# One-bank PSUM tiles, P·V in runs of three, and new costs in the planner of an LSH-attention and feed-forward kernel

## The chip, the cores and the metric

The kernel runs on one core of a Trainium2 chip. The metric is the device time of one execution in microseconds (us), less is better. Before the change it is 746.21 us, the median of three runs (745.81 to 746.28).

The engines are named as in the profile: PE is TensorE, which multiplies matrices (PEld is its loading of weights); DVE is VectorE, ACT ScalarE, POOL GpSimd; SP issues DMAs. Each engine works through its own list of instructions in order. PSUM is the memory that PE writes to; it has eight banks, and here one bank holds 512 float32 numbers in each of 128 partitions.

## The reference

Two batches of eight heads of hashed attention (768 tokens, 64 numbers a head), then two feed-forward layers over all 1536 tokens, 512 wide with 2048 hidden numbers:

```
q_bits = (einsum("bhsd,dk->bhsk", q, proj) > 0); likewise k_bits      # 6 bits: a bucket
mask   = q_bucket[:, :, :, None] == k_bucket[:, :, None, :]
scores = where(mask, q @ k.T / sqrt(64), -1e9)
attn   = exp(scores - max);  attn = attn / (sum + 1e-9)
x      = (attn @ v) put back to (1536, 512)
x      = maximum(0.01 * h, h) @ w_out     with h = x @ w_in           # layer 1
x      = (maximum(h, 0) + alpha * minimum(h, 0)) @ w_out              # layer 2
```

All inputs and the output are float32.

## The kernel before

Attention goes over eight pairs of heads. Of each pair there are twelve scores, each 128 queries by 768 keys: four matmuls (L708, `sc`) fill a PSUM tile of two banks, DVE takes the minimum with a fill value and the row's minimum (L715), ACT the exponential (L718), PE turns the result over in pieces of three 128x128 blocks (L734, `pp`), and ACT copies these out (L739, `pt`). Two such PSUM tiles of two banks each (`s_ps`) take turns. P times V follows in two halves of a pair, each of six chunks (one for each 128 keys): a chunk is six float16 matmuls (L805) and two or four float32 ones (L814), all summed into one bank. In the plan each chunk is an operation of its own, which the planner may put anywhere.

The feed-forward products are computed in float16 halves: each float32 operand is split into a high and a low part, and a product is three matmuls, high x high, high x low, low x high (L1169, L1170, L1171, the function `three`), here called a triple. Hidden products `h` take two triples per 384 tokens. Where a layer's weights allow it (`fast`) seven products p1 to p7 stand for eight (a Strassen scheme); then some results are sums of two PSUM results, which DVE makes (`sum_up`, L1214). Output groups `y` (`y_group`) take four triples; DVE then adds the group to x (L1303; the first of four groups is copied by ACT, L1300). The float16 halves of weights, of x and of the hidden values come from ACT (casts and scaled copies), DVE (L1094, `high x scale - low`) and POOL (L414, subtractions).

After attention the two score tiles of two banks get a second use: half 0 of each is a bank for `y` (`y_banks`), half 1 a bank for p2 and for the maxima that set scales (`b_banks`). To find such a scale DVE reduces to one number per partition, ACT or POOL puts these on a diagonal (`dg`, L619), PE turns them into rows (L948), and DVE takes the maximum (L952) and makes a power of two.

The order of the work isn't written by hand. Every operation is put in a `Plan` with its claim (a coarse place in the order), the engines that could do it with a duration on each, and what it reads and writes. `Plan.order` runs a list scheduler forwards for six values of `PATIENCE`, then seven passes back and forth each, and keeps the shortest plan. `hop` is what it takes from the end of one operation to the start of one that depends on it: 0.12 us, or 0.29 us behind PE, nothing within an engine. The plan only sets the order of each engine's instructions (and which engine does what); the waits between engines are semaphores that the framework puts in from the program's order and the tiles that each instruction touches.

The second layer begins with new float16 halves of x: x (`x_keep`, L1094) and sums of its quarters (L1155), seven operands in all, for each batch.

Of the kernel before, what the change touches and what calls it, by code (L numbers as in the profile page):

```python
# [9 lines left out]
F32 = mybir.dt.float32  # L10
# [26 lines left out]
HOP, HOP_PE, LANDING = 0.12, 0.29, 1.6  # L37
# [5 lines left out]
LAG = 6  # L43
X_LEAD, CONV = 30, (2, 5, 19, 6)
# [10 lines left out]
class Buf:  # L55
# [12 lines left out]
    def put(self):  # L68

        if not self.ring:  # L70
            return None
        if self.slot:
            assert self.slot.bufs[-1] is self, self.slot.tag
            return None
        self.slot = self.ring.next()
        self.slot.bufs.append(self)
        return self.slot.bufs[-2] if len(self.slot.bufs) > 1 else None


class Ring:  # L80


    def __init__(self, slots):
        self.slots, self.n = list(slots), 0
# [8 lines left out]

class Op:
# [34 lines left out]
class Lines(dict):  # L129
# [9 lines left out]
    def soonest(self, op, last=False):  # L139

        best = None
        for k, way in enumerate(op.ways):
            eng, dur, port, _ = way
            at = 0.0
# [3 lines left out]
            if last:  # L148
                at = max([at] + [line.ends[-1] for line in lines if line.ends])
            else:  # L150
                while (then := max(line.early(at, dur) for line in lines)) > at + 1e-9:
                    at = then
# [10 lines left out]
    def latest(self, way, start, done):  # L163
# [4 lines left out]
        at, lines = min(start, done - dur), self.of(way)  # L168
        while (then := min(line.late(at + dur, dur) for line in lines)) < at - 1e-9:
            at = then  # L170
        return at, at + dur, 0.0

    def put(self, way, at, x):
        for line in self.of(way):
            line.put(at, way[1])
# [128 lines left out]
def lsh_attention_ffn_kernel(  # L304
# [177 lines left out]
    def split_qk(i, parts):  # L482
        for nm, hi, at in (("k", 1, -15), ("q", 0, -13)):
# [3 lines left out]
            for part in range(parts):  # L487
# [31 lines left out]
                lo_ways = [vec(0.9 * u + 0.05, d_lo, True), gps(1.75 * u + 0.05, p_lo)]  # L519
# [4 lines left out]
    def turn(i):  # L524
# [3 lines left out]
        for nm, hi, sc in (("k", 64, -scale), ("q", 0, 1.0)):  # L528
            n = st_nat.pop((nm, i))
            for j in range(2):  # L530
                a, bb = ops[j][nm + "a"], ops[j][nm + "b"]
                for f in range(2):
# [10 lines left out]
                    plan.add(at, pe(0.33, go), [(n, (j, j + 1)), ident], [ps])  # L543
# [27 lines left out]
    def bits(i):  # L571
        bt = bt_r.new([128, S], F32, "bt")
        at = 12 * i - 6
        for f in range(2):
# [11 lines left out]
            plan.add(at, pe(0.7, go), [(s, (f, f + 1)) for s in sides] + [lhs], [ps])  # L586
# [30 lines left out]
    def diagonal(out, by):  # L617
        return [
            act(0.33, lambda: nc.scalar.activation(  # L619
# [4 lines left out]
    def split_v(i):  # L624
# [20 lines left out]
        plan.add(at, pe(0.2, lambda: nc.tensor.matmul(  # L645
# [3 lines left out]
        def scales():  # L649
# [8 lines left out]
        plan.add(at, vec(0.9, scales), [ps], [c, (inv, (i, i + 1))])  # L658
# [10 lines left out]
            [vec(1.25, lambda: nc.vector.scalar_tensor_tensor(  # L669
# [22 lines left out]
    def score(g):  # L692
# [21 lines left out]
        plan.add(g - 1, pe(0.71, go), [o[a] for a in op_r], [sc])  # L714
# [3 lines left out]
        plan.add(g, act(1.12, lambda: nc.scalar.activation(  # L718
# [4 lines left out]
        if hi_eng == "T":  # L723
            for h in range(2):
# [6 lines left out]
                def over(ps=ps, h=h):  # L731
# [4 lines left out]
                plan.add(g + 1 + h / 2, pe(0.33, over), [s, ident], [ps])  # L736
                w = [(pt, (t * 64 + 2 * c0, t * 64 + 2 * (c0 + TH)))]
                plan.add(g + 1 + h / 2, [
                    act(0.49, lambda ps=ps, out=out: nc.scalar.copy(out=out(), in_=ps.t)),  # L739
# [9 lines left out]
        if lo_eng == "P":  # L749
            plan.add(g + 1, gps(1.0, lambda: gmul(s.t, s.t, PSCALE)), [s], [s])  # L750
            by = 1.0
        ways = {"A": act(0.84, lambda: nc.scalar.mul(hi(), s.t, by)),
                "P": gps(0.84, lambda: gmul(hi(), s.t, by))}
        plan.add(g + 1, [ways["A"]] if lo_eng == "P" and not FH else list(ways.values()), [s], [hw])
        if lo_eng == "P":
            plan.add(g + 2, gps(1.79, lambda: gsub(lo(), s.t, hi())), [s, hw], [lw])
        else:
            plan.add(g + 2, vec(1.02, lambda: nc.vector.scalar_tensor_tensor(
# [10 lines left out]
    def pv(i, f):  # L769
# [7 lines left out]
        plan.add(at, gps(0.2, lambda: nc.gpsimd.tensor_scalar(  # L777
            out=sm.t, in0=sm.t, scalar1=1e-9, scalar2=1.0, op0=ALU.add, op1=ALU.mult)), [sm], [sm])
        plan.add(at, vec(0.22, lambda: nc.vector.reciprocal(out=sm.t, in_=sm.t)), [sm], [sm])
        plan.add(at, gps(0.6, lambda: nc.gpsimd.tensor_scalar(  # L780
# [8 lines left out]
        plan.add(at, pe(0.33, along), [rb, ident], [pr])  # L789
# [11 lines left out]
        for c in range(T):  # L801
            def go(c=c):
                for n, (piece, o) in enumerate(((0, 0), (1, 0), (0, T))):
                    for j in range(2):
                        nc.tensor.matmul(  # L805
                            ps.t[64 * j:64 * j + 64, 0:split],
                            lhsT=vb.t[:, piece, j, c, :],
                            rhs=narrow(pt, i, f)[:, 2 * T * j + o + c],
                            start=(c + n == 0), stop=(c == T - 1 and n == 2),
                            skip_group_check=True,  # L810
                        )
                for t in range(split // 128, TH):
                    for j in range(2):
                        nc.tensor.matmul(  # L814
                            ps.t[64 * j:64 * j + 64, t * 128:t * 128 + 128],
                            lhsT=v32.t[:, j, c, :], rhs=whole(pt, t)[:, T * j + c],
                            start=False, stop=(c == T - 1), skip_group_check=True,
                        )

            plan.add(at + c / 4, pe(0.55 + 0.025 * (TH - split // 128), go), [vb, pt, v32], [ps])  # L820
# [101 lines left out]
    def power(claim, cols_, most, most_use, scale_, scale_use, extra=None, reads=(), writes=(), wide=False, to=2.0**13):  # L922
# [23 lines left out]
        plan.add(claim, vec(0.5 if wide else 0.35, diag), [buf], [mx, buf] if wide else [mx])  # L946
# [478 lines left out]
```

## Time and profile before

| | |
|---|---|
| median of the runs | 746.21 us |
| the profiled execution | 746.68 us |
| its span, first to last instruction | 744.7 us |
| mean granted clock of TensorE | 0.990 |
| PE busy | 709.6 us, 95% of the span |
| DVE busy | 605.3 us, 81% |
| ACT busy | 479.9 us, 64% |
| POOL busy | 305.3 us, 41% |
| chain that ended last | PE 77%, DVE 15%, ACT 3% |

Times below are from the span's start. Attention lasts until about 247 us, the first layer until about 480, the second from there to the end. A matmul's end is modelled in the records, so matmuls that follow one another closely overlap in them: the pace is the distance between starts. "Idle before, releaser" is the time for which the engine had nothing before an instruction, and the instruction that then let it go.

### The profile page before, as it was taken

The page shows a single profiled execution, that of the slowest core. Times are in us where ns is not written, and L with a number is a line of the kernel's source. Part 1 is how long each engine was busy: PE and PEld are TensorE (multiplying, and loading weights), DVE is VectorE, ACT ScalarE, POOL GpSimd, SP SyncE. Part 2 cuts the span into 40 slices and gives each one's busy share as a digit, 9 for nine tenths or more (in the row PEclk, how much of TensorE's full clock was granted, in tenths as well). Part 3 has the DMA queues.
Part 4 walks back from the last instruction along what each step waited for, and adds up shares of the span by engine and source line. Part 5 has one row for each costly group of instructions (what it writes and reads, how often), then busy time and mean ns, then how long its engine had stood idle before and what let it go on. Part 6 is the DMA issues. An engine that isn't in the chain of part 4 may idle for free.

```text
span 744.7 us, 13170 instructions
## 1 busy us (share of the span) xinstructions
PE 709.6 (95%) x4979; PEld 452.8 (61%) x4979; DVE 605.3 (81%) x1097; ACT 479.9 (64%) x907; POOL 305.3 (41%) x313
## 2 busy tenths in 40 slices
PE   7999999999995999999999999988999999999997
PEld 5778787788774665565565566554555555454443
DVE  6978787767989966789898879899989999788442
ACT  6988777788888675775656555654767655555430
POOL 2987756666373242141452224233133334221420
PEclk9999999999997999999999999999999999999999
DMA  7596686777757230330231313020032113010012
GB/s 212 132 207 155 159 196 149 153 156 132 119 121 198 85 114 1 114 114 28 86 114 58 101 70 114 28 85 2 22 107 99 57 58 114 1 56 1 28 43 99
DMA packets 109488, 72.41 MB, mean 97 GB/s; under 512 B 79137, under 2 KB 101665, under 8 KB 109425
## 3 DMA queue, kind: packets, MB, share of 16 engines
q1 hardware_dynamic: 109424, 71.57, 36.4%
q8 instruction: 39, 0.64, 0.4%
q14 instruction: 25, 0.20, 0.1%
HBM read 43.00 MB, written 3.15 MB: 62 GB/s over the span
## 4 chain that ended last, share of the span: by engine, by line
PE 77%; DVE 15%; ACT 3%; issue 2%; POOL 1%; DMA 1%; DVEq 0%; POOLq 0%; ACTq 0%
PE y L1169 11%; PE y L1171 11%; PE y L1170 11%; PE h L1169 8%; PE h L1171 8%; PE h L1170 8%; PE sc L708 7%; PE pp L734 4%; PE o L805 4%; PE o L814 4%; DVE ff L1094 3%; PE tp L537 2%; DVE s L715 2%; DVE x L1303 1%; PE bp L580 1%
## 5 line engine op out<-in xcount | busy, mean ns | idle before, releaser
L414 POOL TENSOR_TENSOR ff<-ff 128x384 f16<-128x384 f32 x128 | 136.3, 1079 | 323.6 <-ACT ff L1203 214.4
L1169 PE MATMUL y<-ff 128*128 128x384 f16 (+1 forms) x496 | 172.0, 347 | 8.7 <-DVE ff L1214 3.4
L1171 PE MATMUL y<-ff 128*128 128x384 f16 (+1 forms) x496 | 171.8, 346 | 0.0
L1170 PE MATMUL y<-ff 128*128 128x384 f16 (+1 forms) x496 | 171.8, 346 | 0.0
L1170 PEld LDWEIGHTS <-ff 128*128 128x128 f16 x912 | 89.2, 98 | 81.3 <-issue 15.2
L1169 PE MATMUL h<-ff 128*128 128x384 f16 x416 | 135.7, 326 | 2.4 <-DVE ff L1200 2.4
L1170 PE MATMUL h<-ff 128*128 128x384 f16 x416 | 135.6, 326 | 0.6 <-DVE ff L1094 0.6
L1171 PE MATMUL h<-ff 128*128 128x384 f16 x416 | 135.6, 326 | 0.0
L1171 PEld LDWEIGHTS <-ff 128*128 128x128 f16 x912 | 89.2, 98 | 70.0 <-issue 0.8
L1169 PEld LDWEIGHTS <-ff 128*128 128x128 f16 x912 | 89.2, 98 | 69.1 <-DVE biggest L952 0.8
L715 DVE TENSOR_SCALAR_CACHE_REDUCE s<-sc 128x768 f32<-128x768 f32 x96 | 90.3, 954 | 24.9 <-PE sc L708 19.4
L718 ACT ACTIVATE s<-s,mn 128x768 f32<-128x768 f32 x96 | 89.8, 937 | 4.5 <-DVE s L715 4.2
L1203 ACT CAST ff<-ff 128x384 f16<-128x384 f32 x128 | 64.8, 511 | 26.1 <-DVE ff L1200 24.2
L1303 DVE SCALAR_TENSOR_TENSOR x<-y,back,x 128x384 f32<-128x384 f32 (+1 forms) x84 | 55.8, 669 | 31.4 <-PE y L1171 30.5
L1210 ACT COPY ff<-h 128x384 f32<-128x384 f32 x72 | 34.3, 476 | 52.1 <-PE h L1171 51.2
L739 ACT COPY pt<-pp 128x384 f32<-128x384 f32 x96 | 45.6, 475 | 24.9 <-PE pp L734 24.4
L708 PE MATMUL sc<-ka,qa 128*128 128x384 f32 x192 | 56.9, 377 | 2.6 <-DVE s L715 2.4
L734 PE MATMUL pp<-ident,s 128*128 128x128 f32 x288 | 50.9, 286 | 4.2 <-ACT pt L739 3.4
L1094 DVE SCALAR_TENSOR_TENSOR ff<-ff,by 128x512 f16<-128x512 f32 (+2 forms) x54 | 50.6, 970 | 0.7 <-ACT ff L1092 0.7
L708 PE MATMUL sc<-kb,qb 76*128 76x384 f32 x192 | 49.8, 340 | 0.6 <-ACT kb L611 0.6
L1092 ACT ACTIVATE ff<-ff,by 128x512 f16<-128x512 f32 (+2 forms) x54 | 44.2, 865 | 6.8 <-DVE by L957 4.3
L814 PE MATMUL o<-pt,v 128*64 128x128 f32 x576 | 48.4, 276 | 0.0
(141 smaller groups left out, 1199.4 us busy)
## 6 DMA issues: line engine op xcount, KB each, us to landing
ff<-in_moe_w_in_dram SPq DMA_DIRECT2D x32, 512.0 KB
ff<-in_moe_w_out_dram SPq DMA_DIRECT2D x32, 512.0 KB
v<-in_v_dram SPq DMA_DIRECT2D x8, 384.0 KB
out_dram<-x SPq DMA_DIRECT2D x12, 256.0 KB
k<-in_k_dram SPq DMA_DIRECT2D x7, 384.0 KB
q<-in_q_dram SPq DMA_DIRECT2D x7, 384.0 KB
kb<-ka SPq DMA_DIRECT2D x14, 192.0 KB
qb<-qa SPq DMA_DIRECT2D x14, 192.0 KB
```

The costliest lines, as they stand in the source:

```text
L414: nc.gpsimd.tensor_tensor(out=o, in0=a, in1=b, op=ALU.subtract)
L708: nc.tensor.matmul(sc.t[:, h, 0:HALF], lhsT=o[a].t[0:rows, row:row + 128], rhs=o[b].t[0:rows, h * HALF:h * HALF + HALF], start=(n == 0), s ...
L715: plan.add(g, vec(1.03, lambda: nc.vector.tensor_scalar(out=s.t.rearrange("p (a b) -> p a b", a=2), in0=sc.t[:, :, 0:HALF], scalar1=FILL, ...
L718: plan.add(g, act(1.12, lambda: nc.scalar.activation(out=s.t, in_=s.t, func=AF.Exp, scale=-1.0, bias=mn.t[:, 0:1], accum_out=sm.t[:, t, j: ...
L734: nc.tensor.transpose(ps.t[:, c], s.t[:, k0:k0 + 128], ident.t)
L814: nc.tensor.matmul(ps.t[64 * j:64 * j + 64, t * 128:t * 128 + 128], lhsT=v32.t[:, j, c, :], rhs=whole(pt, t)[:, T * j + c], start=False, s ...
L1094: plan.add(claim, vec(0.2 + w * 0.00108, lambda: nc.vector.scalar_tensor_tensor(out=part(lo), in0=src(), scalar=c(), in1=part(hi), op0=ALU ...
L1169: nc.tensor.matmul(ps, lhsT=lh[0], rhs=rh[0], start=first, stop=False, skip_group_check=skip)
L1170: nc.tensor.matmul(ps, lhsT=lh[0], rhs=rh[1], start=False, stop=False, skip_group_check=skip)
L1171: nc.tensor.matmul(ps, lhsT=lh[1], rhs=rh[0], start=False, stop=last, skip_group_check=skip)
L1203: plan.add(claim, act(0.51, lambda: nc.scalar.copy(out=gh.ap(), in_=g.ap(F32))), [g.use()], [gh.use()])
L1303: plan.add(claim, vec(0.69 if l else 0.56, lambda: nc.vector.scalar_tensor_tensor(out=a(), in0=ps.ap(w), scalar=c(), in1=a(), op0=ALU.mult ...
```

## The change

There are three parts.

PSUM: the score tiles come from a pool of their own, which is released when the feed-forward part begins. In its place four separate tiles of one bank each are allocated (`f_at`): two for `y`, two for p2 and the maxima. Each of them waits for all uses of the score tiles (`Whole`).

P times V: three chunks of a half are now one operation of the plan, so that PE does them without anything between.

The planner: durations are other numbers (most by some hundredths of a microsecond); the hop depends on the engine that waits, 0.03 to 0.08 us, with 0.2 us (`DRAIN`) more behind PE; an operation holds its engine for less than it lasts (`OVERLAP`, `held`), by 0.1 us on ACT, 0.082 on DVE, 0.038 on POOL.

```diff
-HOP, HOP_PE, LANDING = 0.12, 0.29, 1.6
+HOP, LANDING = {"DVE": 0.034, "ACT": 0.034, "POOL": 0.08, "PE": 0.054, "SP": 0.03}, 1.6
+OVERLAP = {"ACT": 0.1, "DVE": 0.082, "POOL": 0.038, "PE": -0.0}
+DRAIN = 0.2
...
+RUN, PV0 = 3, 0.22
...
+class Later:
...
+    def tile(self, *args, **kw):
+        self.pool = self.pool or self.make()
+        return self.pool.tile(*args, **kw)
...
+def held(way):
+    return max(way[1] - OVERLAP.get(way[0], 0.0), 0.05)
...
 def hop(one, other):
-    return 0.0 if one[0] == other[0] != "SP" else HOP_PE if one[0] == "PE" else HOP
+    if one[0] == other[0] != "SP":
+        return held(one) - one[1]
+    return HOP[other[0]] + (DRAIN if one[0] == "PE" else 0.0)
...
-    s_ps = ring("ps_s", 2, space=PSUM)
...
+    s_pool = tc.alloc_tile_pool(name="ps_s", bufs=1, space=PSUM)
+    s_ps = Ring([Slot(s_pool, f"ps_s{k}") for k in range(2)])
+
+    def single():
+        s_pool.release()
+        return ctx.enter_context(tc.tile_pool(name="ps_f", bufs=1, space=PSUM, reuse_waits="tile"))
+
+    f_pool = Later(single)
...
-        plan.add(g, vec(1.03, lambda: nc.vector.tensor_scalar(
+        plan.add(g, vec(0.965, lambda: nc.vector.tensor_scalar(
...
-            plan.add(at + c / 4, pe(0.55 + 0.025 * (TH - split // 128), go), [vb, pt, v32], [ps])
+        for c0 in range(0, T, RUN):
+            def go(c0=c0):
+                for c in range(c0, c0 + RUN):
+                    chunk(c)
+
+            plan.add(at + c0 / 4, pe(PV0 + RUN * (0.485 + 0.061 * (TH - split // 128)), go), [vb, pt, v32], [ps])
...
-    s_at2 = [part(s_ps, k).new([128, 2, 512], F32, "y") for k in range(2)]
-    y_banks = Slots([Bank(b, 0) for b in s_at2])
-    b_banks = Slots([Bank(b, 1) for b in s_at2])
+    f_at = [Ring([Slot(f_pool, f"ps_f{k}")], Whole(s_ps)).new([128, 512], F32, "y") for k in range(4)]
+    y_banks, b_banks = (Slots([Bank(b, 0) for b in f_at[k:k + 2]]) for k in (0, 2))
```

The first place where instructions move is PE in the feed-forward part, at a p2 (the tile `y_3630` in before, `y_3639` after). Before, these were its two triples; `y_3630` is the two-bank tile, of which p2 fills half 1, and the `y` group just ahead had filled half 0:

```order
L1169 LDWEIGHTS ff_3702
L1169 MATMUL y_3630<-ff_3200,ff_3702 128x384
L1170 LDWEIGHTS ff_3702
L1170 MATMUL y_3630<-ff_3200,ff_3702 128x384
L1171 LDWEIGHTS ff_3702
L1171 MATMUL y_3630<-ff_3200,ff_3702 128x384
L1169 LDWEIGHTS ff_3702
L1169 MATMUL y_3630<-ff_3200,ff_3702 128x384 [waits DVE_49]
```

The wait in the last row is on the DVE instruction that reads half 0. After, in the place that answers to it:

```order
L1212 LDWEIGHTS ff_3680
L1212 MATMUL y_3639<-ff_3181,ff_3680 128x384 [waits DVE_49]
L1213 LDWEIGHTS ff_3680
L1213 MATMUL y_3639<-ff_3181,ff_3680 128x384
L1214 LDWEIGHTS ff_3680
L1214 MATMUL y_3639<-ff_3181,ff_3680 128x384
L1212 LDWEIGHTS ff_3680
L1212 MATMUL y_3639<-ff_3181,ff_3680 128x384
```

The only wait on DVE stands at the first triple, and is for the reader that emptied this same bank; the second triple waits for nothing. In the whole program 38 matmuls into these tiles waited for a reader of the other half; none does after.

The second place is PE in attention, at a half of P times V (`o`; a chunk ends with its L814 row, L853 after). Before:

```order
L814 MATMUL o<-pt,v 64x128 x4
...
L814 MATMUL o<-pt,v 64x128 x4
L734 MATMUL pp<-ident,s 128x128 x3
L805 LDWEIGHTS vb
...
L814 MATMUL o<-pt,v 64x128 x4
...
L814 MATMUL o<-pt,v 64x128 x4
L734 MATMUL pp<-ident,s 128x128 x3
L805 LDWEIGHTS vb
...
L814 MATMUL o<-pt,v 64x128 x4
L708 MATMUL sc<-ka,qa 128x384 x2
```

Here the chunks stand in runs of two, two and one. After:

```order
L853 MATMUL o<-pt,v 64x128 x4
...
L853 MATMUL o<-pt,v 64x128 x4
...
L853 MATMUL o<-pt,v 64x128 x4
L774 MATMUL pp<-ident,s 128x128 x3
L844 LDWEIGHTS vb
...
L853 MATMUL o<-pt,v 64x128 x4
...
L853 MATMUL o<-pt,v 64x128 x4
...
L853 MATMUL o<-pt,v 64x128 x4
L774 MATMUL pp<-ident,s 128x128 x3
L748 MATMUL sc<-ka,qa 128x384 x2
```

Three chunks, one `pp`, three chunks. Over the program 53 runs become 27 (22 of three chunks and five of six).

The third place is DVE at the boundary of the two layers, from the scale of the second layer's input to the first hidden result that needs it (L1200, after L1243). Before:

```order
L1094 SCALAR_TENSOR_TENSOR ff<-ff,side_by 128x512 x2
L1094 SCALAR_TENSOR_TENSOR ff<-x_0_122,y_by,ff 128x768 x2
L1094 SCALAR_TENSOR_TENSOR ff<-x_1_123,y_by,ff 128x768 x2
L1155 TENSOR_TENSOR x_1_123<-x_1_123 128x768
L1155 TENSOR_TENSOR x_1_123<-x_1_123,x_0_122 128x768
L1155 TENSOR_TENSOR x_0_122<-x_1_123,x_0_122 128x768
L1094 SCALAR_TENSOR_TENSOR ff<-x_1_123,y_by,ff 128x768 x2
L1094 SCALAR_TENSOR_TENSOR ff<-x_0_122,y_by,ff 128x768
L1155 TENSOR_TENSOR x_0_122<-x_0_122 128x768
L1200 SCALAR_TENSOR_TENSOR ff<-h,high_by,ff 128x384 x2
```

After:

```order
L1137 SCALAR_TENSOR_TENSOR ff<-ff,side_by 128x512
L1358 TENSOR_REDUCE ym<-x_0_124 128x1
L1137 SCALAR_TENSOR_TENSOR ff<-x_0_122,y_by,ff 128x768 x2
L1137 SCALAR_TENSOR_TENSOR ff<-x_1_123,y_by,ff 128x768 x2
L1198 TENSOR_TENSOR x_1_123<-x_1_123 128x768
L1198 TENSOR_TENSOR x_1_123<-x_1_123,x_0_122 128x768
L1198 TENSOR_TENSOR x_0_122<-x_1_123,x_0_122 128x768
L1137 SCALAR_TENSOR_TENSOR ff<-x_1_123,y_by,ff 128x768 x2
L1243 SCALAR_TENSOR_TENSOR ff<-h,high_by,ff 128x384
```

One weight conversion, one conversion of x and one sum of x have gone from ahead of the first hidden result to behind it; a reduction (L1358), which stood ahead of all these rows before, has come between.

## Rows read from the trace of the kernel before

**Rows 1.** Windows: length, busy time and count of each engine, PEclk, DMA.
```profile
15.00:216.00 201.00, 194.84 (x1908) 157.59 (x1909) 164.17 (x357) 165.52 (x359) 137.44 (x137) 1.00 0.71 155
216.00:247.00 31.00, 22.36 (x252) 17.91 (x252) 28.98 (x56) 24.53 (x43) 11.33 (x9) 0.78 0.64 174
474.00:517.00 43.00, 37.59 (x219) 21.02 (x217) 41.17 (x73) 23.10 (x36) 13.52 (x15) 1.00 0.16 50
560.00:600.00 40.00, 40.00 (x216) 21.00 (x215) 38.86 (x61) 25.50 (x47) 15.45 (x13) 1.00 0.21 73
```
**Rows 2.** Waits of PE, 247 to 744 us: total, times, longest.
```profile
PE y L1169 <- DVE ff L1214: 3.4, 5, 0.7
PE y L1169 <- DVE x L1303: 3.1, 5, 1.0
PE y L1169 <- DVE biggest L952: 1.1, 3, 0.4
PE y L1169 <- DVE y_max L952: 0.4, 1, 0.4
```
**Rows 3.** Timeline of PE and DVE near 422 us: start, duration, [idle before].
```profile
422.11 0.33 PE L1171 MATMUL y<-ff 128*128 128x384 f16 x1
423.14 0.32 PE L1169 MATMUL y<-ff 128*128 128x384 f16 x1 [0.71 <-DVE x L1303]
423.30 0.32 PE L1170 MATMUL y<-ff 128*128 128x384 f16 x1
...
422.47 0.62 DVE L1303 SCALAR_TENSOR_TENSOR x<-y,back,x 128x384 f32<-128x384 f32 x1 [1.52 <-PE y L1171]
```
**Rows 4.** Timeline of PE: a wait in the second layer.
```profile
513.70 0.38 PE L1169 MATMUL y<-ff 128*128 128x512 f16 x1 [0.97 <-DVE x L1303]
```
**Rows 5.** Timeline of PE in attention, chunks between other work.
```profile
217.24 0.52 PE L805 MATMUL o<-pt,vb 128*64 128x256 f16 x6
...
217.91 0.55 PE L734 MATMUL pp<-ident,s 128*128 128x128 f32 x3
218.38 0.52 PE L805 MATMUL o<-pt,vb 128*64 128x256 f16 x6
...
220.28 0.52 PE L805 MATMUL o<-pt,vb 128*64 128x256 f16 x6
...
220.85 0.49 PE L805 MATMUL o<-pt,vb 128*64 128x256 f16 x6
...
222.04 0.55 PE L734 MATMUL pp<-ident,s 128*128 128x128 f32 x3
222.35 0.59 PE L708 MATMUL sc<-ka,qa 128*128 128x384 f32 x2
```
**Rows 6.** Waits of PE, 15 to 216 us.
```profile
PE sc L708 <- DVE s L715: 2.4, 6, 0.8
```
**Rows 7.** Timeline of DVE at the boundary of the layers.
```profile
480.13 1.40 DVE L1094 SCALAR_TENSOR_TENSOR ff<-ff,side_by 128x512 f16<-128x512 f32 x2
...
488.02 2.87 DVE L1094 SCALAR_TENSOR_TENSOR ff<-x,y_by,ff 128x768 f16<-128x768 f32 x3
490.81 0.95 DVE L1155 TENSOR_TENSOR x<-x 128x768 f32<-128x768 f32 x1
491.68 1.14 DVE L1200 SCALAR_TENSOR_TENSOR ff<-h,high_by,ff 128x384 f32<-128x384 f32 x2
```
**Rows 8.** Timeline of PE there.
```profile
482.52 0.32 PE L1170 MATMUL h<-ff 128*128 128x384 f16 x1 [0.58 <-DVE ff L1094]
...
492.35 0.32 PE L1169 MATMUL h<-ff 128*128 128x384 f16 x1 [2.03 <-DVE ff L1200]
```
**Rows 9.** Waits of PE, 216 to 247 us.
```profile
PE y L948 <- ACT dg L619: 5.8, 1, 5.8
```
**Rows 10.** Groups of the page: busy, mean ns of one, idle before.
```profile
L414 POOL TENSOR_TENSOR ff<-ff 128x384 f16<-128x384 f32 x128 | 136.3, 1079 | 323.6 <-ACT ff L1203 214.4
L715 DVE TENSOR_SCALAR_CACHE_REDUCE s<-sc 128x768 f32<-128x768 f32 x96 | 90.3, 954 | 24.9 <-PE sc L708 19.4
```

More of the change, by code (lines that the diff above doesn't have):

```diff
@@ L143, in soonest @@
             eng, dur, port, _ = way
+            use = held(way)
             at = 0.0
@@ L150, in soonest @@
             else:
-                while (then := max(line.early(at, dur) for line in lines)) > at + 1e-9:
+                while (then := max(line.early(at, use) for line in lines)) > at + 1e-9:
                     at = then
@@ L167, in latest @@
             return self["SP"].late(min(start, x - dur / 2) + dur, dur), x + port + LANDING, x
-        at, lines = min(start, done - dur), self.of(way)
-        while (then := min(line.late(at + dur, dur) for line in lines)) < at - 1e-9:
+        at, lines, use = min(start, done - dur), self.of(way), held(way)
+        while (then := min(line.late(at + use, use) for line in lines)) < at - 1e-9:
             at = then
@@ L174, in put @@
         for line in self.of(way):
-            line.put(at, way[1])
+            line.put(at, held(way))
         if way[0] == "SP":
@@ L585, in bits @@
             sides = [st_op[i][j][nm + "a"] for j in range(2) for nm in "qk"]
-            plan.add(at, pe(0.7, go), [(s, (f, f + 1)) for s in sides] + [lhs], [ps])
+            plan.add(at, pe(0.785, go), [(s, (f, f + 1)) for s in sides] + [lhs], [ps])
             plan.add(
@@ L800, in pv, with chunk @@
         v32 = st_v32[i]
[L801 to L818, printed above, removed]
-            plan.add(at + c / 4, pe(0.55 + 0.025 * (TH - split // 128), go), [vb, pt, v32], [ps])
+        def chunk(c):
+            for n, (piece, o) in enumerate(((0, 0), (1, 0), (0, T))):
+                for j in range(2):
+                    nc.tensor.matmul(
+                        ps.t[64 * j:64 * j + 64, 0:split],
+                        lhsT=vb.t[:, piece, j, c, :],
+                        rhs=narrow(pt, i, f)[:, 2 * T * j + o + c],
+                        start=(c + n == 0), stop=(c == T - 1 and n == 2),
+                        skip_group_check=True,
+                    )
+            for t in range(split // 128, TH):
+                for j in range(2):
+                    nc.tensor.matmul(
+                        ps.t[64 * j:64 * j + 64, t * 128:t * 128 + 128],
+                        lhsT=v32.t[:, j, c, :], rhs=whole(pt, t)[:, T * j + c],
+                        start=False, stop=(c == T - 1), skip_group_check=True,
+                    )
+        for c0 in range(0, T, RUN):
[3 more added lines that the diff above has]
+            plan.add(at + c0 / 4, pe(PV0 + RUN * (0.485 + 0.061 * (TH - split // 128)), go), [vb, pt, v32], [ps])
         plan.add(at + T / 4, vec(0.56, lambda: nc.vector.tensor_tensor(
@@ L944, in diag @@
             )
-        plan.add(claim, vec(0.5 if wide else 0.35, diag), [buf], [mx, buf] if wide else [mx])
+        plan.add(claim, vec(0.53 if wide else 0.37, diag), [buf], [mx, buf] if wide else [mx])
         plan.add(claim, diagonal(dg, mx), [mx, ident], [dg_])
@@ L959, in scales @@
                 extra()
-        plan.add(claim, vec(1.2 if extra else 1.0, scales), [ps.use(), *reads], [most_use, scale_use, *writes])
+        plan.add(claim, vec(0.98 if extra else 0.855, scales), [ps.use(), *reads], [most_use, scale_use, *writes])
     def convert(n, *args):
@@ L1289, in y_group @@
         for j in range(FQ):
-            plan.add(claim, pe(0.64 if l else 0.485, lambda j=j: go(j)),
+            plan.add(claim, pe(0.648 if l else 0.488, lambda j=j: go(j)),
                      [a.use() for a in (*ws[j], *gg[j])], [ps.use()])
```

86 lines of the change are left out of this document (47 added, 39 removed).

## The prediction, made before the changed kernel ran

> **What bounds the kernel now.** I read the windows by stage first. PE is busy in 194.84 of 201 us of attention, in 22.36 of the 31 us that follow (there at a granted clock of 0.78), in 37.59 of 43 us around the boundary of the layers, and in all of 40 us in a piece of the second layer [rows 1]. So PE bounds the kernel and every gain must come out of a stall of PE or a gap between its matmuls. DVE is next: 38.86 of 40 us in a stretch where PE never stops. Then I read the waits of PE after attention, and asked of each which bank its matmul writes and which bank the reader empties.
>
> The reader should see in [rows 3] that the wait at 423.14 stands inside a product: its first triple ended with the matmul at 422.11, and the second is held until DVE's L1303, which began at 422.47, is through. L1303 reads the `y` in half 0, the product is written to half 1. The semaphore is there because both halves are one tile. The order shows the same for 38 matmuls. Most had no effect, since the reader was long done; the stalls of [rows 2] are those where it wasn't.
>
> A stall costs more than its idle time. The matmul after 423.14 starts 0.16 us later, though each is shown with 0.32 us: they overlap, and a stall ends the overlap. From 422.11 to 423.14 are 1.03 us, 0.87 more than the pace, where the view says 0.71 of idle time. So I add 0.16 for each stall.
>
> The Trainium skill, in "Perfetto Trace Analysis" (Tensor Engine Instruction), says that a matmul's end in a trace is worked out from its size and not observed. By the ends the false waits would be worth 7.0 us, by the starts, which the trace measures, 9.1; the sum below goes by starts.
>
> **One-bank tiles.** Waits on L1214, L1303 and the two reductions after a maximum come to 3.4 + 3.1 + 1.1 + 0.4 = 8.0 us in 14 stalls [rows 2]. One, the 0.97 at 513.70 [rows 4], is in the order a wait on its own bank and stays out: 7.0 us in 13, with 13 x 0.16 = 2.1 that is 9.1. One more of the L1303 waits is on its own bank too; without it I take 8.7 us. The order of the changed kernel has no wait across banks. What is late next: the true reader of the same bank. In the order of before 13 waits had under 0.65 us of PE work between the read bank and the waiting matmul; after, in the steady part none has under 1.2 us, because each unit goes four `y` triples, then four of `h`. DVE's lateness at L1303 and L1214 is about the length of one of them (0.62 us in [rows 3]) behind the drain of PE, so 1.2 us mostly covers it. Bounds: 9.1 gained, or 4 if DVE's queue makes half of the true waits late. The releasing of the score pool adds one wait, of the first `y` for the last score's reader, which is over before.
>
> **P times V in runs.** [Rows 5] give the price of cutting a run. A chunk inside a run takes 220.85 - 220.28 = 0.57 us from start to start; the last of one, 217.91 - 217.24 = 0.67, so leaving costs about 0.1. A `pp` before a chunk takes 218.38 - 217.91 = 0.47, a `pp` before a score 222.35 - 222.04 = 0.31, so entering from `pp` costs 0.16. 53 runs become 27 by the order: 26 exits and 26 entries less. Exits: 26 x 0.085 (smaller in halves with four L814 a chunk than the 0.1) = 2.2 us. Entries: 0.16 if all were behind `pp`, but half are behind scores and transposes, which I set at two thirds of it: 26 x 0.11 = 2.8. Together 5.0 us. Bounds: 26 x 0.26 = 6.8 from these rows, 0 if something else waits in attention anyway. PE bounds attention at 97%, so I take 5.0.
>
> What stands against it: PE is away for 222.04 - 220.28 = 1.76 us in a run of three, and DVE's work on one score is 0.954 us [rows 10]. The run at 220.28 is already one of three; `pp` and a score follow it at once. DVE has 201 - 164.17 = 37 us of slack in attention, 1.4 us for each of 27 runs.
>
> **The order of attention.** PE now has 72 waits with under 1.2 us of its own work behind the producer, by the order with the trace's durations, where it had 58. Before, the waits for DVE's L715 stall six times for 2.4 us [rows 6], 0.4 each and 0.16 for the overlap. If 14 more tight waits stall as often as the 58 did, with a fifth of 0.56, that is 1.5 us. I add 1.5. Bounds: -2 (the planner's truer numbers remove the old stalls), +8 (every one stalls).
>
> **The boundary of the layers.** There 5.4 us of 43 go idle [rows 1]. The largest is 2.03 us at 492.35 [rows 8]: an `h` waits for L1200 to empty a bank, and L1200 starts at 491.68 behind all of DVE's work on x [rows 7]. By the order of DVE half of 1.40 (`side_by`), a third of 2.87 (x) and the sum of 0.95 move behind L1200, 2.6 us in all; a reduction that stood ahead comes between, at some 0.5. Against 2.2 us of stall (2.03 + 0.16) that leaves nothing to 0.3: a gain of 2.0. The other two, 0.58 at 482.52 and 0.97 at 513.70 [rows 4, 8], are 0.74 and 1.13 with the overlap; I count 1.5 of 1.9. Gain 3.5 us, bounds 0 and 4.1. What is late next are the remaining two conversions of x, needed by the last product.
>
> **From attention to the first layer.** PE waits 5.8 us for a diagonal [rows 9] and runs the rest at a low clock: 0.78 over 31 us is 13.6 us at the lower of the two levels, 1.2 in place of 2.4 GHz [rows 1]. The change puts 15 triples of `h` ahead of the last six chunks and some weight conversions behind DVE's way to the maximum. From the rows of DVE, added in the new order, the idle time is about 9 us where it was 8.6 (31 - 22.36), and less work falls at the low clock. I take a gain of 1, between 4 lost (maximum late by one chain of conversions) and 4 gained (most of the 5.8).
>
> **Diagonals on POOL.** By the order POOL makes 13 of 16 diagonals in the feed-forward part, where ACT made nearly all. POOL's subtraction L414 takes 1.079 us [rows 10], and a diagonal queued behind one is late by up to that. In the order PE has 7 to 18 us of other work before most of them are needed; two have under 3. I count nothing; without that cover it is 13 x 1.08 = 14 us.
>
> The Trainium skill ("SBUF — State Buffer", Who interferes with whom) says that a POOL instruction that reads SBUF and a DVE instruction with two SBUF inputs shut each other out for the whole instruction. By that rule a diagonal on POOL would also wait for a conversion on DVE, and the sum would be worse by an estimated 13 us more without cover. No row of before shows a diagonal of POOL held up so.
>
> **Sum.** 746.7 (the profiled execution) - 8.7 - 5.0 + 1.5 - 3.5 - 1.0 = 730.0. The median is 0.5 below the profiled execution: 729.5 us.
>
> **Rivals.** (A) Attention gains nothing: the 5.0 and the 1.0 are taken back by tighter waits, as the planner's hops of 0.03 to 0.08 us leave less room than 0.12. For it: 14 more tight waits, DVE and ACT both busy over 80% there. Against: only 2.4 us of stalls on L715 now. Time: 729.5 + 6 = 735.5.
>
> (B) Only the false waits go; boundary, attention and diagonals come out even. 746.2 - 8.7 = 737.5. For it: each of the other terms rests on an order whose timing I worked out myself.
>
> (C) The false waits were a symptom: DVE is late, and the same time is lost at the next true wait. For it: DVE at 38.86 of 40 us [rows 1]. Against: in that very stretch PE doesn't stall. If half of the 8.7 comes back and nothing else is won: 742.
>
> (D) Diagonals late behind L414, without cover: 729.5 + 14 = 743.5. Against: the distances in the order.
>
> (E) Slower: the runs of three starve the two score tiles. While PE is 1.76 us in a run, DVE empties a score in 0.954 us; when only one is filled DVE stands still for 0.8 us, the exponentials behind it too, and PE meets its next score or `pp` with nothing ready. If that costs PE a whole minimum of 0.954 in each of 27 runs it is 26 us: 729.5 + 26 = 755. It decides from 16.7/27 = 0.62 us a run. For it: DVE, ACT and PE are all close to full in attention. Against: the run at 220.28 [rows 5].
>
> **How the numbers follow.** Forecast 0.50, A 0.20, B 0.13, C 0.04, D 0.03, E 0.06, and 0.04 for a time under the forecast's own range of 722 to 734 (gains at the transition and fewer old stalls in attention). From 721 to 741 the forecast, A and B are held, some 0.83. A measurement of this kernel tells 0.2%, 1.5 us, from no change. Faster: forecast, A, B, the low end, and most of C and D: 0.90. The same takes a small share of C, D and E, 0.03; slower is E and bad mixtures, 0.07.
>
> **What would show it.** Right: among the waits of PE after attention no stall of a product's second triple on a reader of another tile, L1169's old waits (now L1212) under 2 us; `pp` before a chunk half as often, and the window that answers to 15 to 216 us shorter by 3 to 5 us; no wait near 2 us on L1243. Wrong: waits of `y` on a diagonal (L659) beyond the first, by POOL (D); waits of `sc` on L755 well over 2.4 us after runs (E); new waits on L1257 and L1346 of the same bank that add up to the old 8 us (C).

## The result and the profile after

The changed kernel takes 733.17 us (median of five runs, 732.99 to 734.17), where the kernel before takes 746.21: a ratio of 0.9831 (0.9817 to 0.9846). The forecast was 729.5 us with a range of 721 to 741. The profiled execution has a span of 731.2 us, 13.5 less; its mean granted clock is 0.987, where it was 0.990.

The windows of the changed kernel, cut at the same times as [rows 1] (length, busy time and count of PE, PEld, DVE, ACT, POOL, then granted clock, DMA share, GB/s):

```profile
15.00:216.00 201.00, 193.00 (x1967) 162.64 (x1965) 173.52 (x362) 166.71 (x361) 144.48 (x140) 0.99 0.73 158
216.00:247.00 31.00, 21.20 (x168) 14.27 (x166) 29.41 (x61) 23.36 (x42) 10.02 (x10) 0.78 0.60 164
474.00:517.00 43.00, 41.92 (x247) 23.96 (x245) 41.69 (x69) 25.81 (x39) 13.72 (x14) 1.00 0.16 50
```

Around the boundary of the layers PE is now busy for 41.92 of 43 us (37.59 before). In the stretch behind attention nothing improved: 21.20 us of 31, the clock again 0.78. In attention PE does more matmuls (1967 for 1908) in the same 201 us, and is idle a little longer, 8.0 us for 6.2.

All waits of PE behind attention, from 244 us to the end (total, times, longest), the answer to [rows 2]:

```profile
PE y L991 <- POOL dg L451: 1.6, 3, 1.1
PE h L1212 <- DVE ff L1257: 1.2, 3, 0.7
```

No wait of a `y` tile's matmul (L1212) on L1257, L1346 or a reduction is left; the rest are waits of `h` on its own bank and waits for diagonals. Before, the same view had, beside [rows 2], these lines, which the boundary mostly makes:

```profile
PE h L1169 <- DVE ff L1200: 2.4, 2, 2.0
PE y L948 <- ACT dg L619: 1.0, 1, 1.0
PE h L1170 <- DVE ff L1094: 0.6, 1, 0.6
PE y L1169 <- ACT x L1300: 0.5, 1, 0.5
```

That is 12.5 us of idle time in 19 stalls before, and 2.8 in 6 after. At the boundary, DVE of the changed kernel, the answer to [rows 7]:

```profile
472.57 0.29 DVE L995 TENSOR_REDUCE y_max<-y 128x1 f32<-128x128 f32 x1 [0.44 <-PE y L991]
...
473.55 0.74 DVE L1137 SCALAR_TENSOR_TENSOR ff<-ff,side_by 128x512 f16<-128x512 f32 x1
...
474.67 3.79 DVE L1137 SCALAR_TENSOR_TENSOR ff<-x,y_by,ff 128x768 f16<-128x768 f32 x4
...
483.10 0.61 DVE L1243 SCALAR_TENSOR_TENSOR ff<-h,high_by,ff 128x384 f32<-128x384 f32 x1
```

From the maximum to the start of the first hidden result are 10.5 us, and no wait of PE on L1243 is in the list any more; the 2.03 us of [rows 8] are gone.

Attention is the other side. The waits of PE from 15 to 216 us (to set against [rows 6]), and then from 216 to 247 us, against [rows 9]:

```profile
PE sc L748 <- DVE s L755: 4.7, 6, 1.8
PE pp L774 <- ACT pt L779: 1.6, 4, 0.7
PE pp L774 <- ACT s L758: 0.9, 2, 0.5
...
PE pp L774 <- ACT pt L779: 5.7, 4, 4.2
PE y L991 <- POOL dg L451: 2.7, 1, 2.7
PE h L1212 <- ACT ff L1135: 1.1, 1, 1.1
...
```

Scores wait 4.7 us for DVE where it was 2.4. Of these, 3.2 us stand before 27 us (1.3 before), while the first chunk of P times V starts only at 38.3 us, so runs of chunks can't have made them. The diagonal's 5.8 us became 2.7, but 5.7 us of waits for ACT's copies (`pt`) came to stand beside it. The 301st matmul of the feed-forward part starts at 295.29 us (295.69 before), and from there to the end are 435.93 us (449.05 before): the feed-forward part gained what was forecast, and attention with the transition gained 0.4 us.

### The profile page after: what moved, and what is told of

Read it like the earlier page. It is cut to its first block, busy times and chain, and to the rows that moved or that the text cites. A ratio compares the mean times of both kernels' runs of the same rounds, so it can differ in the third digit from the quotient of the medians.

```text
span 731.2 us, 13167 instructions
## 1 busy us (share of the span) xinstructions
PE 702.8 (96%) x4979; PEld 454.5 (62%) x4979; DVE 610.9 (84%) x1095; ACT 475.5 (65%) x891; POOL 320.9 (44%) x331
## 4 chain that ended last, share of the span: by engine, by line
PE 73%; DVE 17%; ACT 4%; issue 3%; POOL 1%; DMA 1%; SPq 1%; POOLq 0%; DVEq 0%; ACTq 0%
PE y L1212 10%; PE y L1213 10%; PE y L1214 10%; PE h L1212 7%; PE h L1214 7%; PE h L1213 7%; PE sc L748 7%; PE pp L774 4%; PE o L853 3%; PE o L844 3%; DVE ff L1137 3%; PE tp L577 2%; DVE x L1346 2%; ACT s L758 1%; DVE ff L1050 1%
## 5 line engine op out<-in xcount | busy, mean ns | idle before, releaser
L1212 PE MATMUL y<-ff 128*128 128x384 f16 (+1 forms) x496 | 172.0, 347 | 0.0
L1212 PE MATMUL h<-ff 128*128 128x384 f16 x416 | 136.8, 329 | 2.5 <-DVE ff L1257 1.2
L1212 PEld LDWEIGHTS <-ff 128*128 128x128 f16 x912 | 89.4, 98 | 70.4 <-ACT ff L1135 1.5
L1346 DVE SCALAR_TENSOR_TENSOR x<-y,back,x 128x384 f32<-128x384 f32 (+1 forms) x84 | 56.3, 670 | 31.3 <-PE y L1214 31.1
L779 ACT COPY pt<-pp 128x384 f32<-128x384 f32 x96 | 45.6, 475 | 23.2 <-PE pp L774 22.9
L774 PEld LDWEIGHTS pp<-ident,s 128*128 128x128 f32 x288 | 32.9, 143 | 24.2 <-ACT pt L779 14.2
```

The lines of the kernel that those rows point to most:

```text
L774: nc.tensor.transpose(ps.t[:, c], s.t[:, k0:k0 + 128], ident.t)
L779: act(0.478, lambda ps=ps, out=out: nc.scalar.copy(out=out(), in_=ps.t)),
L1212: nc.tensor.matmul(ps, lhsT=lh[0], rhs=rh[0], start=first, stop=False, skip_group_check=skip)
L1346: plan.add(claim, vec(0.748 if l else 0.61, lambda: nc.vector.scalar_tensor_tensor(out=a(), in0=ps.ap(w), scalar=c(), in1=a(), op0=ALU.mul ...
```

## The experiments

The first five and the last keep an order of instructions fixed, so that one thing alone changes. The other kernels go through the planner again, and their orders differ everywhere.

**One-bank tiles alone, on the order of before.**

```diff
-    s_ps = ring("ps_s", 2, space=PSUM)
+    s_pool = tc.alloc_tile_pool(name="ps_s", bufs=1, space=PSUM)
+    s_ps = Ring([Slot(s_pool, f"ps_s{k}") for k in range(2)])
...
+    f_pool = Later(single)
...
-    s_at2 = [part(s_ps, k).new([128, 2, 512], F32, "y") for k in range(2)]
-    y_banks = Slots([Bank(b, 0) for b in s_at2])
-    b_banks = Slots([Bank(b, 1) for b in s_at2])
+    f_at = [Ring([Slot(f_pool, f"ps_f{k}")], Whole(s_ps)).new([128, 512], F32, "y") for k in range(4)]
+    y_banks, b_banks = (Slots([Bank(b, 0) for b in f_at[k:k + 2]]) for k in (0, 2))
```

> The kernel before with one-bank tiles alone; the order of every engine is that of before, instruction for instruction. If the 13 stalls on readers of the other half were false waits and nothing else is late, 8.7 us go: 737.5 us. If they were a symptom of a late DVE (rival C), at least half comes back at the next true wait: 742 us or more. The stalls at the boundary of the layers (2.0 and 0.6 us idle) and on the diagonals should stay.

Measured: 737.54 us (737.26 to 737.83), 0.9882 of before (0.9861 to 0.9903): 8.8 us gained of 8.7 expected. All its waits of PE from 247 us on:

```profile
PE h L1197 <- DVE ff L1228: 2.4, 2, 2.0
PE y L976 <- ACT dg L648: 1.4, 2, 1.0
PE h L1198 <- DVE ff L1122: 0.3, 1, 0.3
PE y L1197 <- DVE x L1331: 0.2, 1, 0.2
PE y L1197 <- ACT x L1328: 0.2, 1, 0.2
```

The waits on L1228, 2.0 us and the small one, are those of L1200 before. Of the waits of `y` (L1197) only those on the true reader are left, 0.4 us. Laid beside before, instruction by instruction, the matmuls of the 13 stalls come 9.2 us closer to the ones ahead of them: 7.07 us of idle time and 13 x 0.16. The false waits were a loss by themselves, and DVE didn't take it back; rival C falls.

Two other things in this trace go opposite ways. The wait on the true reader [rows 4] falls from 0.97 to 0.24 us, 0.7 more gained. And behind the stall of 2.03 us at the boundary the granted clock is 0.51 from 488.0 to 491.3 us, where before had 1.00 behind the same stall; that costs some 1.6 us.

**Two-bank tiles again, on the order of the changed kernel.**

```diff
-    f_at = [Ring([Slot(f_pool, f"ps_f{k}")], Whole(s_ps)).new([128, 512], F32, "y") for k in range(4)]
-    y_banks, b_banks = (Slots([Bank(b, 0) for b in f_at[k:k + 2]]) for k in (0, 2))
+    f_at = [Ring([Slot(f_pool, f"ps_f{k}")], Whole(s_ps)).new([128, 2, 512], F32, "y") for k in range(2)]
+    y_banks, b_banks = (Slots([Bank(b, k) for b in f_at]) for k in (0, 1))
```

> The changed kernel with its four one-bank tiles made into two tiles of two banks again; the order of every engine is that of the changed kernel. 56 matmuls wait for a reader of the other half then. Laid on the changed kernel's trace, 21 of these readers end after the matmul has started, by 11.2 us in all. Theory: up to that much slower, 742 us (739 to 745). Rival: the new order spaces writers and readers, so that the width of a tile no longer matters: 734 us.

Measured: 749.45 us (748.96 to 751.35), 1.0045 of before (1.003 to 1.006). Its waits of PE from 244 us:

```profile
PE y L1212 <- DVE ff L1257: 9.1, 12, 1.4
PE y L991 <- POOL dg L451: 2.1, 2, 1.1
PE y L1212 <- DVE x L1346: 2.1, 3, 0.7
PE y L1212 <- DVE biggest L995: 1.5, 4, 0.4
PE y L1212 <- DVE y_max L995: 0.8, 2, 0.4
```

The same tiles cost 16.3 us on this order and 8.8 on the old one, more than expected: 21 waits of `y`, 13.5 us idle, and 0.16 for each. The order of the changed kernel counts on banks being free one by one; without the tiles the kernel would be slower than before. The expectation of 742 (739 to 745) took only readers that end late in a trace without these waits, 11.2 us, and left out the lost overlap, 21 x 0.16 = 3.4. That each stall moves the work behind it, and with it other readers, may account for the 13.5 us of idle time in place of 11.2; no run tests it.

**Runs of chunks alone, on the order of before.** The plan is that of before; when it is emitted, the second and third chunk of each three are put next to the first.

```diff
     def emit(self):
-        for op in self.order():
-            op.ways[op.way][3]()
+        for op in ops:
+            key = self.run_of.get(id(op))
+            for one in ([op] if key is None else runs[key] if key not in done else []):
+                one.ways[one.way][3]()
+            done.add(key)
```

> The kernel before, where only the chunks of P times V move: the second and third of each three are drawn up to the first on PE, all else stands in the old order on all engines. Forecast for runs: 5.0 us less, 741.2 us; by a sum of the prices between starts in both traces 7 us less, 739 us. If the runs of three starve the score tiles (rival E), 746 us or more, with waits of sc on DVE well over 2.4 us.

Measured: 753.02 us (750.97 to 753.98), 1.0085 of before (1.006 to 1.011), so 6.7 us slower, on the side of rival E. The waits of PE from 15 to 216 us:

```profile
PE sc L717 <- DVE s L724: 4.6, 8, 1.4
PE pr L796 <- POOL rb L789: 1.7, 1, 1.7
PE pp L743 <- ACT pt L748: 1.6, 5, 0.6
PE tp L546 <- ACT ka L561: 1.0, 3, 0.5
...
```

One place shows why. PE of the kernel before, and then of this one, between the same two scores:

```profile
207.88 0.52 PE L708 MATMUL sc<-kb,qb 76*128 76x384 f32 x2
208.33 0.36 PE L805 MATMUL o<-pt,vb 128*64 128x128 f16 x6
208.52 0.61 PE L814 MATMUL o<-pt,v 128*64 128x128 f32 x8
209.05 0.62 PE L708 MATMUL sc<-ka,qa 128*128 128x384 f32 x2
```

```profile
210.74 0.52 PE L717 MATMUL sc<-kb,qb 76*128 76x384 f32 x2
212.62 0.62 PE L717 MATMUL sc<-ka,qa 128*128 128x384 f32 x2 [1.35 <-DVE s L724]
```

Before, two chunks filled the time in which DVE emptied a score tile. Drawn together with earlier ones they leave PE with nothing to do for 1.35 us. To weigh the two I took the distances between the starts of successive matmuls up to the third-last score. The price of a step is the 30th percentile of that distance, over the traces, for the same three kinds of matmul in a row; what a step takes above its price is its loss. The prices add up to 5.8 us less than before, near the forecast of 5.0, and the losses to 10.8 more. Some 1.6 of the 10.8 are a loss of clock: right behind the wait shown, from 213.6 to 217.0 us, the granted clock is 0.50.

**Both edits on the order of before.**

```diff
+    f_at = [Ring([Slot(f_pool, f"ps_f{k}")], Whole(s_ps)).new([128, 512], F32, "y") for k in range(4)]
...
+            for one in ([op] if key is None else runs[key] if key not in done else []):
+                one.ways[one.way][3]()
```

> Both edits on the order of before: one-bank tiles and chunks drawn together, no change of the planner's numbers. If the two add up, 746.2 - 8.7 - 5 to 7 = 731 to 732.5 us, as fast as the changed kernel (733.2), and then the new numbers of the planner bring nothing in sum: what they gain at the boundary (3 to 4 us) they lose in attention. If the planner's part is a gain in sum, this one is slower than 734 us.

Measured: 740.57 us (740.34 to 741.83). That is 12.4 less than the runs alone and 3.0 more than the tiles alone. In the traces the two edits simply add up: the 301st feed-forward matmul starts at 300.02 us, with the tiles alone at 295.58, and behind it both take 439.88 us. So the changed kernel's 733.2 isn't these two edits: 7.4 us come from its plan.

**All six chunks in one run, on the order of before, with one-bank tiles.**

```diff
-            plan.run_of[id(plan.ops[-1])] = (i, f, c // 3)
+            plan.run_of[id(plan.ops[-1])] = (i, f)
```

> As the kernel with both edits on the order of before (740.6 us), but all six chunks of a half drawn up to the first: 16 runs in place of 29, all else in the old order. If runs starve the score tiles the longer the run, the stalls of attention grow by more than the 13 x 0.2 us of switches: 743 us or more, and then the 729 us of six chunks in the plan are the planner's doing. If what hurts is only that chunks come earlier than planned: 738 to 741 us.

Measured: 751.33 us (750.23 to 752.07), 10.8 more than with runs of three, though there are 13 fewer runs. Its waits of PE from 20 to 222 us, two lines:

```profile
PE pp L772 <- ACT pt L777: 6.6, 14, 0.8
PE sc L746 <- DVE s L753: 3.4, 6, 1.2
```

On a fixed order longer runs starve PE, first of copies: from the 13th score to the third-last, a stretch at full clock in both traces, are 191.4 us, with runs of three 183.7. The rest of the 10.8 isn't clearly starvation, since before 260 us this trace has 20.4 us at the lower clock and that of runs of three 10.2.

**Runs and numbers in the planner's hands.** Beside the changed kernel stand one with single chunks, and one of before with the tiles and runs of three but the old numbers:

```diff
-RUN, PV0 = 3, 0.22
+RUN, PV0 = 1, 0.22 / 3
```

> The changed kernel with one chunk of P times V per operation of the plan again (tiles and the planner's numbers stay); 47 runs of chunks in place of 27. If the planner, unlike the fixed order of the run before, turns longer runs into a gain, this one is slower by the 20 x 0.2 us of entries and exits: 737 us. If longer runs cost in late scores what they save in switches (rival A), it is the same as the changed kernel or faster: 730 to 733 us, with fewer stalls of pp and sc.

```diff
+            plan.add(at + c0 / 4, pe(RUN * (0.55 + 0.025 * (TH - split // 128)), go), [vb, pt, v32], [ps])
```

> The kernel before with one-bank tiles, and runs of three chunks put into the plan with the old numbers (a run lasts three times the old chunk). Beside 737.5 us of the tiles alone it tells the worth of runs in the planner's hands without the new numbers. Runs are a gain: 733 us. They are even or a loss: 737 to 743 us, and then what the changed kernel has below 737.5 comes from the planner's numbers.

All four with one-bank tiles:

| | single chunks | runs of three |
|---|---|---|
| old numbers | 737.5 | 740.0 (739.07 to 741.28) |
| new numbers | 738.1 (737.28 to 738.68) | 733.2 |

Neither helps the total alone; together they give 4.4 us. The traces show where. Each column is the time in us from the mark before it, read from the starts of PE's matmuls in one trace of each kernel (there are 96 scores, and the 13th is the first of the second pair of heads):

| | start to 13th score | to third-last score | to 301st feed-forward matmul | to the end |
|---|---|---|---|---|
| before | 38.4 | 180.6 | 76.6 | 449.1 |
| tiles alone | 38.4 | 180.5 | 76.7 | 439.9 |
| old numbers, runs of three | 39.4 | 180.5 | 78.2 | 439.1 |
| new numbers, single chunks | 46.2 | 179.2 | 76.2 | 435.2 |
| changed kernel | 43.1 | 175.1 | 77.1 | 435.9 |

With the new numbers the last stretch is 3 to 5 us shorter in these traces, with runs and without (in that of the tiles alone 1.6 us are the lower clock named above). Runs of three take 4.1 us off the second stretch, but only where the numbers are new. And with the new numbers the 13th score comes 4.7 us later, or 7.8 with single chunks, which hides half of the gain or all of it.

**The old hops, without overlap.**

```diff
-HOP, LANDING = {"DVE": 0.034, "ACT": 0.034, "POOL": 0.08, "PE": 0.054, "SP": 0.03}, 1.6
-OVERLAP = {"ACT": 0.1, "DVE": 0.082, "POOL": 0.038, "PE": -0.0}
-DRAIN = 0.2
+HOP, LANDING = {"DVE": 0.12, "ACT": 0.12, "POOL": 0.12, "PE": 0.12, "SP": 0.12}, 1.6
+OVERLAP = {}
+DRAIN = 0.17
```

> The changed kernel with the old hops (0.12 us, 0.29 behind PE) and no overlap on an engine, but the new durations, tiles and runs. If tight hops make the new stalls in attention (rival A: 6 us more of stalls than before, by the distances between starts), this one gets most back there: 728 to 730 us. If the hops are what gave the boundary of the layers and attention their order, it is slower: 736 us or more.

Measured: 733.49 us (733.25 to 733.68), 0.9835 of before (0.9819 to 0.9852), the same as the changed kernel. Its waits of PE from 15 to 250 us begin with

```profile
PE pp L774 <- ACT pt L779: 11.5, 11, 4.1
PE sc L748 <- DVE s L755: 3.0, 6, 0.8
```

Scores wait less, copies more. Neither expectation held. The second stretch of the table takes 175.0 us here and the last 435.4, as in the changed kernel: the new hops and the overlap aren't needed for the gain, so in this plan it is the new durations that count. In this one plan the old hops don't remove the stalls of attention either.

**Runs of two, runs of six, and more search.** Each is one line of the changed kernel.

```diff
-RUN, PV0 = 3, 0.22
+RUN, PV0 = 2, 0.22 * 2 / 3
```

> The changed kernel with runs of two chunks. If the length of a run trades switches against late scores, this stands between one and three: within 2 us of the changed kernel. If the differences between plans are chance (any small change of the planner's input moves the time by some us), it stands outside the times of one and three.

Measured: 734.34 us (732.97 to 736.21), between one and three, as the first expectation has it; so is the second stretch, 177.0 us between 179.2 and 175.1.

```diff
-RUN, PV0 = 3, 0.22
+RUN, PV0 = 6, 0.22
```

> The changed kernel with all six chunks of a half in one run (17 runs or fewer in place of 27). If fewer switches win in the planner's hands throughout, 10 x 0.2 = 2 us less: 731 us. If longer runs (3.5 us, longer than DVE's work on three scores) starve the score tiles, 735 us or more, with waits of sc over 5 us.

Measured: 729.05 us (728.03 to 729.91), 0.9777 of before (0.9761 to 0.9794): faster than both kernels. All its waits of PE from 245 us on, then the largest of attention, from 15 to 219 us:

```profile
PE h L1212 <- DVE ff L1257: 0.5, 1, 0.5
PE y L991 <- ACT dg L659: 0.5, 1, 0.5
PE y L991 <- POOL dg L451: 0.4, 1, 0.4
...
PE sc L748 <- DVE s L755: 4.1, 6, 1.4
PE pp L774 <- ACT pt L779: 2.8, 6, 0.9
```

The same runs of six that cost 13.8 us on the old order (751.3 against 737.5) cost nothing when the planner knows of them: the second stretch takes 174.9 us, as with runs of three. That six are better isn't shown. Of the 3.7 us between the two profiled executions, 2.2 lie behind the 301st feed-forward matmul, where there are no chunks.

```diff
-PATIENCE, PASSES = (0.05, 0.1, 0.15, 0.2, 0.25, 0.3), 7
+PATIENCE, PASSES = tuple(0.02 * k for k in range(1, 31)), 15
```

> The changed kernel, where the planner tries 30 values of patience and 15 passes for 6 and 7, and keeps the plan that is shortest by its own numbers. If its numbers now rank plans as the chip does, the time falls by about what the plan does (2 us): 731 us. If they don't, it lands anywhere within 3 us of 733.

Measured: 737.19 us (736.88 to 738.98). With the same numbers a plan that the planner holds for shorter is 4 us slower on the chip, a little more than the 3 expected of chance. The second stretch is again 175.0 us; the first is 3.1 us longer than in the changed kernel and the last 1.8.

**Diagonals on ACT, all else in the changed kernel's order.**

```diff
     def emit(self):
         for op in self.order():
-            op.ways[op.way][3]()
+            op.ways[0 if id(op) in self.on_act else op.way][3]()
```

> The changed kernel with the feed-forward diagonals that its plan gave to POOL made by ACT, each at the same place in the program; PE and DVE keep their order to the instruction. In the changed kernel's trace PE waits 4.3 us for diagonals of POOL (2.69 after attention, 1.08 at 505.22, where the diagonal took 1.20 us beside DVE's L1053 and 0.37 elsewhere). If POOL is what makes them late: 1.0 to 1.5 us less, 732 us, and the wait at 505.22 under 0.4. The 2.69 stays, since POOL waited for DVE there. Rival: behind ACT's casts they come later still: 734 us or more.

Measured: 732.88 us, but from 731.14 to 737.51: no difference that these runs can show. The place is clear in the trace, though. The changed kernel near 504 us, then this one:

```profile
503.71 1.22 DVE L1053 SCALAR_TENSOR_TENSOR ff<-ff 128x1024 int32<-128x1024 int32 x1
...
503.97 1.20 POOL L451 TENSOR_SCALAR dg<-ident,mx 128x128 fp32r<-128x128 f32 x1 [0.65 <-DVE mx L976]
...
505.22 0.33 PE L991 MATMUL y<-dg,ones 128*128 128x128 f32 x1 [1.08 <-POOL dg L451]
```

```profile
502.24 1.22 DVE L1054 SCALAR_TENSOR_TENSOR ff<-ff 128x1024 int32<-128x1024 int32 x1
...
502.41 0.40 ACT L659 ACTIVATE dg<-ident,mx 128x128 fp32r<-128x128 f32 x1 [1.00 <-DVE mx L976]
...
502.87 0.33 PE L992 MATMUL y<-dg,ones 128*128 128x128 f32 x1
```

On POOL the diagonal ends 0.24 us after DVE's instruction; on ACT it takes 0.40 us beside the same instruction, and PE's matmul comes 0.46 us after ACT began. The rival has its place too: at 471.11 us PE waits 1.11 us for a diagonal on ACT that stood behind 1.40 us of its casts, where on POOL the wait was 0.25. That gives most of it back. Most of the 1.9 us between the profiled executions of the two kernels arises before 27 us, where the changed kernel had a stretch at the lower clock and this one none.

## Why the prediction was right, and where it wasn't

Of the 16.7 us forecast 13.0 came. The feed-forward part gave what its terms said; the terms of attention and the transition, 4.5 us together, gave 0.4.

**Tiles: right, in size too.** 8.7 us were forecast and 8.8 measured on an unchanged order. Two readings carried it: asking of each wait which bank is read and which is written; and adding the lost overlap, 0.16 us a stall [rows 3]. By the idle time alone it would have been 7.0; the 13 stalls gave 9.2, and the working before its last subtraction had 9.1. That the total is 8.8 is in part luck: the 0.4 taken off for a second true reader had no counterpart, as no other wait on L1303 (now L1331) is left, and the true wait at 513.70 [rows 4], which was left out, shrank as well while clock was lost.

**The feed-forward part as a whole: right.** Tiles and boundary were forecast at 12.2 us. PE's waits there fall by 9.7 us in 13 stalls, which with 0.16 each is 11.8; the losses by starts fall by 12.8. The 2.0 us on L1200, which the tiles alone leave, is gone in the changed kernel's order. For the boundary 3.5 were forecast, and 11.8 - 8.8 = 3.0 remain for it, by the starts 4.0. In the 4.0 is the lower clock of the kernel with the tiles alone, some 1.6 us.

**P times V: right in the changed plan, wrong on the old order.** The forecast took 5.0 us off because PE bounds attention at 97%. The switches do cost that: 5.8 by the starts in the kernel where only chunks move. In the changed kernel the gain came: 5.5 us from the 13th score to the third-last, and 175.0 or 175.1 us there in three different plans with runs of three and new durations. But chunks also were what PE did while DVE and ACT were at a score, which the forecast left out. That was rival E's mechanism, at 0.06, and on the old order it is what happens: 10.8 us over 29 runs, 0.37 us a run. The 0.62 at which it would have decided against the whole change isn't reached, but the 0.2 that a run saves is exceeded.

**The order of attention: mis-sized.** Set at +1.5 us. By the starts, the losses up to the third-last score are 58.9 us in the changed kernel and 53.3 before, 5.6 more, while the prices add up to 6.4 less (roughly, since the two orders don't have quite the same work behind that point). So attention comes out nearly even, which was rival A's sum for it, and the changed kernel at 733.2 stands between the forecast and A (735.5). A's reason isn't borne out, however: with the old hops the time is the same. Nor is it the runs: 4.9 of the 5.6 are lost before the 13th score. The forecast spread tight waits over all of attention and missed its beginning. There PE waits three times for DVE, 3.2 us, and the longest wait stands behind a weight conversion (L1047):

```profile
23.16 2.40 POOL L454 TENSOR_TENSOR kn<-k,kn 128x768 fp32r<-128x768 f32 x1
...
23.80 2.04 DVE L1047 TENSOR_SCALAR ff<-ff 128x512 int32<-128x512 int32 x1
...
26.77 0.62 PE L748 MATMUL sc<-ka,qa 128*128 128x384 f32 x2 [1.81 <-DVE s L755]
```

The conversion took 2.04 us where the median of its eight instructions of this size is 0.43. That POOL held it up isn't tested. Some 1.7 us more are clock: the granted clock is 0.50 from 19.5 to 22.9 us (1.00 before), after PE was busy for 2.65 of 4.5 us (3.43 before). The signs that the prediction named for attention didn't come: its window isn't 3 to 5 us shorter (the third-last score starts 0.8 us earlier), and chunks follow a `pp` in 16 places, not in half of the former 21.

**The transition: not gained.** Forecast -1.0, measured +0.4 from the third-last score to the 301st feed-forward matmul. The diagonal's wait is 3.1 us shorter, but PE waits 3.3 us longer for copies of `pt` there, 5.7 us for this line of before, and the clock is again 0.78 over the window:

```profile
PE pp L734 <- ACT pt L739: 2.4, 3, 1.2
```

**Diagonals on POOL: right to count nothing.** Three waits of 1.6 us in the feed-forward part. The longest is the one that the Trainium skill ("SBUF — State Buffer", Who interferes with whom) speaks of: a POOL instruction that reads SBUF is shut out by a DVE instruction with two SBUF inputs. The rows above agree: 1.20 us beside such an instruction, 0.37 in the median of the tile. So do the other diagonals: of the 18 on POOL in the changed kernel, six took 0.73 to 1.72 us, each beside such an instruction, and twelve 0.37 or 0.38. What POOL's diagonals cost in the end isn't settled, as putting them on ACT made no difference that the runs can show.

**What stays open.** By the table the changed kernel is 4.4 us better than the tiles alone because two gains, 5.4 us in the second stretch and 4.0 in the last, outweigh a loss at the beginning. Why the new durations make the first scores later isn't shown, nor why runs of three need them to gain. Plans from the same numbers lie 4 us apart (733.2 and 737.2), and all plans with one-bank tiles between 729.0 and 740.0; the six-chunk kernel's gain over the changed one may be such chance.

## What to carry to other kernels

For each wait of the bounding engine ask whether the instruction waited for touches the same memory; where only a shared tile ties them, split the tile, and count for each stall the idle time and the lost overlap. Work that can go anywhere is filler for an in-order engine: drawing it together saves switches but takes the filler away, so it has to be done in the plan, not after it, and here it paid only in a plan with new durations. To measure one part of a change under a planner, hold the order and change that part alone; two plans with the same numbers can differ by more than the part is worth. Where the order can't be held, compare the traces stretch by stretch: a gain and a loss that hide each other in the total stand apart there.

## What was not expected of the hardware

A diagonal on POOL, 0.37 us in the median, took 1.20 us beside a DVE instruction with two inputs in SBUF and ended 0.24 us after it; the same operation on ACT took 0.40 there. Of the six diagonals on POOL that were held up so, five ended 0.24 us after such an instruction, the longest (1.72 us) 0.15 after.
